# Sliding-window attention and an ELU MLP on one core: q and k turned in 32x32 squares by VectorE and gathered by DMA, v placed by GpSimd

## The chip, the core and the metric

The kernel runs on one core of one Trainium2 chip. A core has a matrix engine (TensorE, PE in the profile; its weight loads are PEld), three engines for elementwise work (VectorE or DVE, ScalarE or ACT, GpSimd or POOL), and SyncE (SP), which here only issues DMAs. Each works through its own queue in order and waits on semaphores for the others. The metric is device time in microseconds of one execution, as the median of several.

## What is computed

```python
B, H, S, D = 8, 8, 576, 64
scores = scale * np.matmul(q, k.transpose(0, 1, 3, 2))        # scale = 1/8
rel = pos[:, None] - pos[None, :]
slopes = 2.0 ** (-8.0 * (np.arange(H) + 1) / H)
bias = slopes[:, None, None] * (-np.abs(rel))[None]
mask = (rel >= 0) & (rel < 128)
scores = np.where(mask, scores + bias[None], -1e9)
attn = softmax(scores)
x = np.matmul(attn, v)                     # to 4608 x 512, heads side by side
h = x @ w_in                               # 512 x 2048
g = np.where(h > 0.0, h, np.exp(np.minimum(h, 0.0)) - 1.0)
out = g @ w_out                            # 2048 x 512
```

A query sees itself and the 127 keys before it, so a block of 128 queries needs its own block of 128 keys and the one before.

## The kernel before

All matmuls take 16-bit inputs. `q` and `k` must be laid with the head dimension on partitions for the scores, so each batch's q and k are turned. They are loaded with a cast by DMAs that GpSimd issues (`load_qk`, line 76): partition p holds the four sequence rows 4p to 4p+3 of all heads, 1 KB at a time. `transposes(b, hp)` (line 307) turns two heads of q and k at a time with eight 128x128 transposes on TensorE into one PSUM tile `tp`, and two copies of 64x1024, on VectorE for even `hp` and on ACT for odd, put them into `QK[b % 2]` (lines 322 and 324). The tile `tp` uses the same two PSUM buffers (pool `ps_s`) as the score tiles. The last 64 rows of a batch are the tail, turned by `transposes_tail` (line 327). Because of the loading by fours, a block of 128 sequence positions stands in QK in the order j, i (position 4i + j), and so do the positions of v in `VP` and the rows of the output.

Partitions 64 to 127 of `QK[i]` hold extra rows (`TQ`, `TK`) by which the same matmul adds the bias and switches off masked groups. For batch 0 a separate matmul adds bias and mask instead. The extra rows are made once during batch 0 (`terms`, `group_rows`, `k_term`) and spread over the heads by DMAs from SP (`fill`, `fill_k`).

v of batches 0 to 2 is loaded like q and k into `vs` in one DMA of 1 KB runs, and `place_v4` (line 114) moves it into `VP` on VectorE, 16 copies of 32x512 a batch. v of batches 3 to 7 is loaded by `load_v` (line 119) from SP, 16 DMAs of 64 KB and one of 128 KB a batch, in runs of 256 bytes that already stand in the right partitions, and `cast_v` (line 132) converts it on GpSimd into `VP`, five instructions a batch.

The program is laid out by hand in steps. Sixteen steps make a batch; step `s` of batch `b` (number 16b + s) runs `scores(b, s)` for one bank of scores, its exponential on ACT (line 372) and, from batch 1 on, the `cut` on VectorE (line 380), which takes the minimum with a band so that masked entries vanish. `values` multiplies the bank of the step before with v (line 394), `normalize` (lines 414 and 415) divides by the sums, and `turn` brings the result into `xT`, for batches 0 and 1 by TensorE and a VectorE copy, from batch 2 on by a DMA transpose that SP issues (line 423). Each step from 4 on also carries one `hidden` group of the MLP: matmuls into one of two PSUM buffers `hp` (line 451), the exponential on ACT (line 455), a clamp on GpSimd (line 456), and in the next step `elu` on VectorE (line 463), which also frees the `hp` buffer. Steps 36 and 37 have no `hidden`. From step 13 on a quarter of an output block follows at the end of each step (`output`, line 492; every fourth step ends in an ACT copy and stores from SP).

Within a step the order on every engine is: `hidden`, the `elu` of the step before, then the tasks listed for the step, then `output`:

```python
        for s in range(max(OUT) + 1):
            if s in HID:
                hidden(*HID[s])
            if s - 1 in HID:
                elu(*HID[s - 1])
            for f, a in tasks.get(s, []):
                f(*a)
            if s in OUT:
                output(*OUT[s])
```

For the preparation of the next batches the tasks of batch b >= 2 are (s0 = 16b): `transposes(b + 1, hp)` at s0 + 5, 9, 10, 13, the tail at s0 + 14; the loads of k and q of b + 2 at s0 + 10 and 12, their tails at 11 and 13; `load_v(b + 2, n)` at s0 + 18 + 2n and `cast_v` three steps later. For b = 1 the transposes are at s0 + 9, 10, 13, 14; for b = 0 at 14, 14, 15, 15. Hence in one steady batch VectorE has per step one `elu`, one `cut` and, in ten of sixteen steps, a normalization, GpSimd one clamp per step beside its DMA issues and casts.

The softmax here doesn't subtract the row's maximum and nothing guards it: scores larger than these inputs give would overflow.

## Time and profile before

| | us |
|---|---|
| median of 7 runs (lowest, highest) | 367.15 (366.21, 368.05) |
| profiled execution | 366.21 |
| its span, first to last instruction | 364.4 |

| longest groups (engine, line, what) | busy us | mean ns |
|---|---|---|
| PE L451, hidden matmuls, x1536 | 150.3 | 246 |
| PE L492, output matmuls, x576 | 146.4 | 379 |
| DVE L463, elu, x144 | 98.0 | 680 |
| POOL L456, clamp, x144 | 88.5 | 614 |
| ACT L455, exponential of the MLP, x144 | 86.0 | 597 |
| ACT L372, exponential of the scores, x128 | 76.0 | 593 |
| DVE L380, cut, x112 | 49.5 | 442 |
| ACT L322, copies of turned q and k, x28 | 28.1 | 1005 |
| POOL L134, casts of v, x25 | 19.5 | 779 |
| DVE L324, copies of turned q and k, x28 | 19.2 | 685 |
| PE L312, transposes of q and k, x224 | 17.1 | 219 |
| DVE L116, placing of v, x48 | 15.1 | 315 |

A row gives the engine, the line of the kernel, the time that instructions of the group were running in all, and the mean of one. Matmuls overlap each other, so the mean of one is longer than its share of the engine's time. The granted TensorE clock was 0.994 of full speed on average. The DMA engines moved 37.06 MB in 81948 packets, 51952 of them under 512 bytes; the queue of DMAs issued by GpSimd took 35.5% of the sixteen engines' time, the one of SP 25.8%.

### The profile page before, as it was taken

The page shows a single profiled execution, that of the slowest core. Times are in us where ns is not written, and L with a number is a line of the kernel's source. Part 1 is how long each engine was busy: PE and PEld are TensorE (multiplying, and loading weights), DVE is VectorE, ACT ScalarE, POOL GpSimd, SP SyncE. Part 2 cuts the span into 40 slices and gives each one's busy share as a digit, 9 for nine tenths or more (in the row PEclk, how much of TensorE's full clock was granted, in tenths as well). Part 3 has the DMA queues.
Part 4 walks back from the last instruction along what each step waited for, and adds up shares of the span by engine and source line. Part 5 has one row for each costly group of instructions (what it writes and reads, how often), then busy time and mean ns, then how long its engine had stood idle before and what let it go on. Part 6 is the DMA issues. An engine that isn't in the chain of part 4 may idle for free.

```text
span 364.4 us, 9613 instructions
## 1 busy us (share of the span) xinstructions
PE 340.4 (93%) x3790; PEld 251.7 (69%) x3790; DVE 243.5 (67%) x574; ACT 206.7 (57%) x349; POOL 145.6 (40%) x229
## 2 busy tenths in 40 slices
PE   6877997999979999999999999999999999999994
PEld 6765874777747767767777777777777777666652
DVE  6479889677886776676677767776776756634430
ACT  4364573567537655765656665676567565543431
POOL 9145624435314733472346424642443223233320
PEclk9899999999999999999999999999999999999999
DMA  8999989849244974497447945694631222211113
GB/s 115 201 205 131 207 100 177 149 91 156 41 95 91 131 112 90 106 127 112 91 106 113 131 91 107 105 142 90 96 84 45 52 47 45 50 40 48 31 43 73
DMA packets 81948, 37.06 MB, mean 102 GB/s; under 512 B 51952, under 2 KB 77296, under 8 KB 81904
## 3 DMA queue, kind: packets, MB, share of 16 engines
q0 software_dynamic: 34064, 15.40, 35.5%
q1 hardware_dynamic: 47840, 21.06, 25.8%
q8 instruction: 29, 0.48, 0.6%
q14 instruction: 15, 0.12, 0.1%
HBM read 36.70 MB, written 9.44 MB: 127 GB/s over the span
## 4 chain that ended last, share of the span: by engine, by line
PE 65%; DVE 13%; ACT 9%; DMA 7%; issue 3%; POOL 1%; SPq 0%; ACTq 0%; POOLq 0%
PE hp L451 28%; PE op L492 25%; PE sp L348 5%; ACT QK L322 5%; DVE VP L116 4%; PE av L394 3%; DMA vs<-in_v_dram 3%; DVE g L463 3%; ACT EX L372 2%; ACT e L455 2%; DMA xT<-xn 2%; DVE QK L324 1%; DVE EX L380 1%; DMA stq<-in_q_dram 1%; PE tp L312 1%
## 5 line engine op out<-in xcount | busy, mean ns | idle before, releaser
L456 POOL TENSOR_SCALAR e<-e 128x512 f32<-128x512 f32 x144 | 88.5, 614 | 201.8 <-ACT e L455 200.3
L451 PE MATMUL hp<-xT,wi 128*128 128x256 f16 (+3 forms) x1536 | 150.3, 246 | 7.9 <-DVE g L463 5.2
L451 PEld LDWEIGHTS <-wi 128*128 128x128 f16 x1536 | 121.6, 98 | 49.6 <-issue 6.9
L455 ACT ACTIVATE e<-hp 128x512 f32<-128x512 f32 x144 | 86.0, 597 | 118.0 <-PE hp L451 109.6
L492 PE MATMUL op<-wo,g 128*128 128x512 f16 x576 | 146.4, 379 | 0.0
L463 DVE SCALAR_TENSOR_TENSOR g<-e,hp 128x512 f16<-128x512 f32 x144 | 98.0, 680 | 23.9 <-POOL e L456 22.7
L380 DVE TENSOR_TENSOR EX<-EX,band 128x512 f16<-128x512 f16 x112 | 49.5, 442 | 57.2 <-ACT EX L372 57.1
L372 ACT ACTIVATE EX<-sp 128x512 f16<-128x512 f32 x128 | 76.0, 593 | 15.0 <-PE sp L368 10.5
L492 PEld LDWEIGHTS <-g 128*128 128x128 f16 x576 | 51.2, 98 | 36.9
L348 PE MATMUL sp<-QK 128*128 128x128 f16 (+3 forms) x576 | 49.8, 213 | 0.4 <-DVE QK L305 0.4
L394 PE MATMUL av<-VP,EX 128*128 128x65 f16 x576 | 38.6, 193 | 4.5 <-DVE EX L380 2.5
L394 PEld LDWEIGHTS <-EX 128*128 128x128 f16 x576 | 31.5, 98 | 9.0 <-DVE EX L380 4.0
L415 DVE TENSOR_TENSOR xn<-av,rden 128x256 f16<-128x256 f32 x80 | 34.0, 424 | 2.8
L348 PEld LDWEIGHTS <-QK 128*128 128x128 f16 (+1 forms) x576 | 31.3, 97 | 1.4 <-DVE QK L305 0.5
L496 ACT COPY ob<-op 128x512 f32<-128x512 f32 x36 | 21.1, 585 | 14.3 <-PE op L492 6.4
L322 ACT COPY QK<-tp 64x1024 f16<-64x1024 f16 x28 | 28.1, 1005 | 1.6 <-PE tp L312 1.4
L414 DVE RECIPROCAL rden<-av 128x4 f32<-128x4 f32 x80 | 14.4, 180 | 16.5 <-PE av L394 15.5
L134 POOL TENSOR_SCALAR VP<-vf 128x512 f16<-128x512 f32 (+1 forms) x25 | 19.5, 779 | 2.4 <-DMA vf<-in_v_dram 2.4
L324 DVE COPY QK<-tp 64x1024 f16<-64x1024 f16 x28 | 19.2, 685 | 1.1 <-PE tp L312 0.9
L312 PE MATMUL tp<-ident,stq 128*128 128x128 f16 x224 | 17.1, 219 | 2.3 <-ACT QK L322 1.0
L312 PEld LDWEIGHTS <-stq 128*128 128x128 f16 x224 | 13.8, 98 | 3.4 <-issue 3.2
L116 DVE COPY VP<-vs 32x512 f16<-32x512 f16 x48 | 15.1, 315 | 1.4 <-DMA vs<-in_v_dram 0.7
(70 smaller groups left out, 117.9 us busy)
## 6 DMA issues: line engine op xcount, KB each, us to landing
out_dram<-ob SPq DMA_DIRECT2D x128, 64.0 KB, 1.7
vf<-in_v_dram SPq DMA_DIRECT2D x80, 64.0 KB, 2.2
stq<-in_k_dram POOLq DMA_DIRECT2D x7, 512.0 KB, 6.4
stq<-in_q_dram POOLq DMA_DIRECT2D x7, 512.0 KB, 7.7
wi<-in_moe_w_in_dram POOLq DMA_DIRECT2D x4, 512.0 KB, 11.6
wo<-in_moe_w_out_dram POOLq DMA_DIRECT2D x4, 512.0 KB, 14.4
QK<-TQ SPq DMA_DIRECT2D x2, 576.0 KB, 8.8
vs<-in_v_dram POOLq DMA_DIRECT2D x2, 512.0 KB, 10.0
```

The source lines that it names most:

```text
L312: nc.tensor.transpose(t[:, g, w, :, j, :], stq[b][:, w, 2 * hp + g, 2 * j:2 * j + 2, :].rearrange("p a d -> p (a d)"), ident)
L322: nc.scalar.copy(o, i)
L348: nc.tensor.matmul(t[:, o:o + n], qk[0:r, h, 1, kc:kc + 128], qk[0:r, h, 0, qc:qc + n], start=b > 0 or o == 0, stop=b > 0)
L372: nc.scalar.activation(e[:, 0:512], t, AF.Exp, scale=0.125)
L380: V.tensor_tensor(out=e, in0=e, in1=band[:, c:c + n].unsqueeze(1).broadcast_to([128, 512 // n, n]), op=ALU.min)
L394: nc.tensor.matmul(a[:, l, :], e[:, c:c + 128], vp[:, n, h, 0:D + 1], start=st, stop=sp)
L415: V.tensor_tensor(out=xnt[b, i][:, 4 * half:4 * half + 4, :], in0=a[:, :, 0:D], in1=r.unsqueeze(2).broadcast_to([128, 4, D]), op=ALU.mult)
L451: nc.tensor.matmul(p[:, l * w + u0:l * w + u1], w_in_sb[:, c, fc * 128:(fc + 1) * 128], xT[:, c, x0:x0 + u1 - u0], start=(c == 0), stop=(c ...
L455: nc.scalar.activation(e, p, AF.Exp)
L456: nc.gpsimd.tensor_scalar(out=e, in0=e, scalar1=1.0, scalar2=0.0, op0=ALU.min, op1=ALU.max)
L463: V.scalar_tensor_tensor(out=gs[t][:, f0:f0 + nf, c0:c0 + w], in0=sh(es.pop((t, j))), scalar=1.0, in1=sh(hps.pop((t, j))), op0=ALU.subtrac ...
L492: nc.tensor.matmul(ops[t], gs[t][:, fc, ts * 128:(ts + 1) * 128], w_out_sb[:, fc, :], start=(fc == 0), stop=(fc == NFC - 1))
```

## The change

For batches 2 to 7 the TensorE transposes of q and k go, with their copies out of PSUM. In their place `squares` transposes on VectorE: the staged tile is turned in 32x32 squares, in eight instructions of 128x512 a batch, into a tile `tt` of which there is one buffer. `collect` then moves the squares by eight DMAs a batch from SP: for block i of 128 positions and each half of the head dimension, 32 partitions of `tt` go to 32 partitions of `QK`, q and k together, in runs of 2 KB. For that `QK` is laid out by block: `[128, 2, 5, H, 128]` instead of `[128, H, 2, 640]`, and the scores, the zero fills and the copies of the transposes that stay (batches 0 and 1, and all tails) follow it.

v of batches 3 to 7 is loaded as for batch 2 (`load_v4`, one DMA from GpSimd, and `load_v4_tail`), and `place_by_pool` moves it into `VP` on GpSimd with 16 instructions of 32x512 a batch, two a step.

The extra rows of `QK[1]` are spread over the heads by five ACT copies of 64x1024 (`fill_q`) and five VectorE copies of 32x1024 (`fill_k`) in steps 10 to 14; `QK[0]` gets its rows by one DMA from `QK[1]` at step 20, in place of three at step 22.

```diff
-    QK = [one([128, H, 2, 640], F16, f"QK{i}") for i in range(2)]
+    QK = [one([128, 2, 5, H, 128], F16, f"QK{i}") for i in range(2)]
...
-    def load_v(b, n):
-    def cast_v(b, n):
+    def place_by_pool(b, n, u):
+        for j in (2 * u, 2 * u + 1):
+            nc.gpsimd.tensor_scalar(
+                out=VP[b % 2][32 * j:32 * j + 32, n, :, 0:D], in0=vs[b][32 * n:32 * n + 32, :, j, :],
+                scalar1=1.0, scalar2=0.0, op0=ALU.mult, op1=ALU.add)
...
-        def fill(i):
-            nc.sync.dma_start(QK[i][64:128, :, 0, 0:576],
-                              TQ[64:128, :].unsqueeze(1).broadcast_to([64, H, 576]))
-            nc.sync.dma_start(QK[i][g_, :, 1, :], TK[g_, :].unsqueeze(1).broadcast_to([32, H, 640]))
-
-        def fill_k(i):
-            nc.sync.dma_start(QK[i][r_, :, 1, :], QK[1 - i][r_, :, 1, :])
+        def fill_q(n):
+            nc.scalar.copy(QK[1][64:128, 0, n, :, :],
+                           TQ[64:128, 128 * n:128 * n + 128].unsqueeze(1).broadcast_to([64, H, 128]))
+
+        def fill_k(n):
+            V.tensor_copy(QK[1][g_, 1, n, :, :],
+                          TK[g_, 128 * n:128 * n + 128].unsqueeze(1).broadcast_to([32, H, 128]))
...
+        def fill_other():
+            nc.sync.dma_start(QK[0][64:128], QK[1][64:128])
...
+        def put(t, o, by_act):
+
+            for odd in range(2):
+                (nc.scalar.copy if by_act else V.tensor_copy)(
+                    o.rearrange("p w n h (a o i) -> p w n h a o i", o=2, i=32)[:, :, :, :, :, odd, :]
+                    .rearrange("p w n h a i -> p w n (h a) i"),
+                    t[64 * odd:64 * odd + 64].rearrange("p w n h a i -> p w n (h a) i"))
...
+        def squares(b, n):
+
+            if b not in tt:
+                tt[b] = stage.tile([128, 2, 2, H, 4, 32], F16, name="tt", tag="tt", bufs=1)
+            w, dh, hs = 1 - n // 4, n // 2 % 2, slice(4 * (n % 2), 4 * (n % 2) + 4)
+            V.transpose(out=tt[b][:, w, dh, hs, :, :].rearrange("p h j i -> p (h j) i"),
+                        in_=stq[b][:, w, hs, :, 32 * dh:32 * dh + 32].rearrange("p h j d -> p (h j) d"))
+
+        def collect(b, n):
+
+            i, dh = n // 2, n % 2
+            nc.sync.dma_start(
+                QK[b % 2][32 * dh:32 * dh + 32, :, i, :, :].rearrange("p w h c -> p w (h c)"),
+                tt[b][32 * i:32 * i + 32, :, dh, :, :, :].rearrange("p w h j i -> p w (h j i)"))
...
             def mm(o, h, kc, qc, n):
-                nc.tensor.matmul(t[:, o:o + n], qk[0:r, h, 1, kc:kc + 128], qk[0:r, h, 0, qc:qc + n],
+                nc.tensor.matmul(t[:, o:o + n], qk[0:r, 1, kc, h, :], qk[0:r, 0, qc, h, 0:n],
...
-                for hp in range(NP):
-                    at(s0 + ((5, 9, 10, 13) if b > 1 else (9, 10, 13, 14) if b else (14, 14, 15, 15))[hp],
-                       transposes, b + 1, hp)
+                for hp in range(NP if b == 0 else 0):
+                    at((14, 14, 15, 15)[hp], transposes, 1, hp)
+                for n in range(8 if b else 0):
+                    at(s0 + (n if b > 1 else 6 + n // 2), squares, b + 1, n)
+                    at(s0 + (8 if b > 1 else 10) + n // 2, collect, b + 1, n)
...
-                for n in range(5):
-                    at(s0 + 18 + 2 * n, load_v, b + 2, n)
-                    at(s0 + 21 + 2 * n, cast_v, b + 2, n)
+                at(s0 + 14, load_v4, b + 2)
+                at(s0 + 19, load_v4_tail, b + 2)
+                for n in range(4):
+                    for u in range(2):
+                        at(s0 + 20 + 2 * n + u, place_by_pool, b + 2, n, u)
...
-        at(10, fill, 1)
+        for n in range(5):
+            at(10 + n, fill_q, n)
+            at(10 + n, fill_k, n)
...
-        at(22, fill, 0)
-        at(22, fill_k, 0)
+        at(20, fill_other)
```

## The prediction

> **What bounds the kernel now.** I read the page first (busy shares), then the table of stretches (how one batch compares with another), then the order in time of a few steps, then the rows of single lines.
>
> ```profile
> PE 340.4 (93%) x3790; PEld 251.7 (69%) x3790; DVE 243.5 (67%) x574; ACT 206.7 (57%) x349; POOL 145.6 (40%) x229
> ```
>
> TensorE is busy nearly always. A share of busy time doesn't say what an edit is worth, so I cut the span into stretches (length, then busy time of PE, PEld, DVE, ACT, POOL, clock, DMA):
>
> ```profile
> 36.00:51.00 15.00, 14.27 (x210) 11.59 (x209) 12.86 (x31) 9.41 (x14) 7.46 (x11) 1.00 1.26 192
> 93.00:112.30 19.30, 16.44 (x194) 11.54 (x193) 15.66 (x43) 8.99 (x16) 4.93 (x11) 1.00 0.34 71
> 209.41:246.18 36.77, 36.31 (x381) 26.73 (x379) 25.95 (x58) 23.58 (x40) 16.64 (x25) 1.00 0.66 111
> 280.79:314.46 33.67, 33.67 (x382) 25.10 (x379) 22.66 (x52) 19.90 (x37) 9.80 (x16) 1.00 0.22 50
> ```
>
> The third row is sixteen steps of the steady loop, with the transposes of one next batch in them; the fourth is sixteen steps of batch 7, which prepares no next batch. Both are bound by TensorE, and the same attention and MLP work takes 36.77 us with the preparation and 33.67 us without. The first two rows (the end of batch 0, the first half of batch 2) have idle TensorE beside a VectorE that is 86% and 81% busy.
>
> A step with transposes and a step after it, in order of time (start, length, engine, line):
>
> ```profile
> 216.68 1.04 PE L451 MATMUL hp<-xT,wi 128*128 128x256 f16 x8
> 217.90 0.61 PE L312 MATMUL tp<-ident,stq 128*128 128x128 f16 x8
> 218.34 1.03 PE L492 MATMUL op<-wo,g 128*128 128x512 f16 x4
> 218.43 0.61 POOL L456 TENSOR_SCALAR e<-e 128x512 f32<-128x512 f32 x1 [1.47 <-ACT e L455]
> 218.87 0.45 DVE L380 TENSOR_TENSOR EX<-EX,band 128x512 f16<-128x512 f16 x1 [1.03 <-ACT EX L372]
> 219.00 0.79 POOL L134 TENSOR_SCALAR VP<-vf 128x512 f16<-128x512 f32 x1
> 219.21 1.04 PE L451 MATMUL hp<-xT,wi 128*128 128x256 f16 x8
> 219.24 1.38 DVE L324 COPY QK<-tp 64x1024 f16<-64x1024 f16 x2
> 221.39 1.03 PE L451 MATMUL hp<-xT,wi 128*128 128x256 f16 x8
> ```
>
> Eight transposes hold TensorE from 217.90 to 218.34, 0.44 us (their 0.61 overlaps the next matmul). The step is 2.53 us (216.68 to 219.21) and the one after, which waits for the two copies on VectorE, 2.18. A step without either is 2.09: the ACT exponentials of the MLP (L455) start at 211.50, 213.59, 215.67, 217.75.
>
> The rows of single lines (min, median and max in ns):
>
> ```profile
> L380 DVE TENSOR_TENSOR EX<-EX,band x112: 415/448/461, 53.7 to 313.4; 128x512 f16<-128x512 f16 x112
> L134 POOL TENSOR_SCALAR VP<-vf x25: 618/789/792, 105.4 to 274.5; 128x512 f16<-128x512 f32 x20, 64x512 f16<-64x512 f32 x5
> L116 DVE COPY VP<-vs x48: 275/285/725, 9.0 to 104.5; 32x512 f16<-32x512 f16 x48
> L322 ACT COPY QK<-tp 64x1024 f16<-64x1024 f16 x28 | 28.1, 1005 | 1.6 <-PE tp L312 1.4
> vf<-in_v_dram SPq DMA_DIRECT2D x80, 64.0 KB, 2.2
> stq<-in_q_dram POOLq DMA_DIRECT2D x7, 512.0 KB, 7.7
> vs<-in_v_dram POOLq DMA_DIRECT2D x2, 512.0 KB, 10.0
> ```
>
> **What the Trainium skill says.** "VectorE: DVE Perf Modes", section "The three transpose paths", gives 311 ns for a 128x128 transpose of 2-byte data in 32x32 blocks on VectorE; the trace has none. "SBUF — State Buffer", section "Who interferes with whom": a VectorE instruction with two SBUF inputs, or in a two-port mode, and a GpSimd instruction that reads SBUF block each other, whoever starts second waits. The trace half agrees: L116, usually 0.285 us, takes up to 0.725, and the GpSimd conversion L134 takes 0.618 alone but 0.79 when it starts just after L380, as at 219.00; L380 itself never goes over 0.461 beside L456. "Perfetto Trace Analysis", section "GPSIMD Engine Instruction", advises timing GpSimd by the spacing of starts; here L134 starts 0.57 us after the L456 whose length is 0.61.
>
> **What goes.** Of batches 2 to 7, 192 transposes with 24 copies on ACT (1.005 us) and 24 on VectorE (0.685). In a steady batch that is worth 36.77 - 33.67 = 3.10, less the tail's transposes, which stay (eight of 64 columns, 0.39 us and a short wait, 0.45 together): **2.65 us**. ACT never sets the pace afterwards. The v loads of batches 3 to 7 (85 DMAs, 17 a batch) leave SP, with 25 GpSimd conversions.
>
> **What comes, part by part.**
>
> Squares: 8 VectorE transposes of 128x512 a batch, 48 in all. Estimate from the page: 311 ns plus 384 more elements at one per cycle of 0.96 GHz is 0.71; the nearest row, L463 with 512 elements, is 0.68. I take 0.70 (0.65 to 0.75). Per batch VectorE gets 5.6 and loses 4 copies, 2.7. That fits overall, but the squares come one a step in the first 8 steps. A step with a normalization holds VectorE from the cut at 210.53 to the end of the xn at 212.27, 1.74 us; with a square 2.44 against 2.09. Five of those eight steps normalize, three don't (1.13 + 0.70 = 1.83): 17.7 us of work in about 16.9. What is late then is the cut (L380), on which the next step's value matmuls wait. It has 0.35 us of idle time before it and about 0.25 after it. Price: 0.3 a batch (0 to 1).
>
> Gather: 8 DMAs a batch on SP, 128 KB each, in rows of 2 KB. Nearest rows: 64 KB in 2.2, 128 KB in 2.9. They are issued four to eight steps (8 us or more) before the first scores that read them. On SP each waits for its squares, with output stores and the xn transposes queued behind; those have several us of room and SP is rid of 17 DMAs. Taken as nothing (0 to 0.5 a batch, if the gather meets the q and k loads).
>
> Placing v: 16 GpSimd instructions of 32x512 in place of 5, two a step in steps 4 to 11 of batches 2 to 6, behind the step's L456. Behind them waits the next L456, then L463, then the matmul that reuses the hp buffer. One costs between 0.57 (spacing) and 0.79: 0.61 + 2 x 0.62 = 1.85 or 0.61 + 2 x 0.79 = 2.19 against 2.09. At the low end it fits. Added to that, in steps 10 and 11 GpSimd issues the k load (0.93) and a tail (0.72): L456 comes some 1.3 us late there. Its room is about 0.9 (the e buffer is ready at 210.70, the matmul that needs its hp starts at 212.51, L463 takes 0.68 and a start). Price 0.4 a batch (0 to 3). The mutual block: with GpSimd nearly always busy, a cut that is late because of a square finds it in a placing and waits up to 0.6; steps 4, 6 and 8 are the ones. Price 0.7 (0 to 1.5).
>
> v's load: one 512 KB DMA issued in step 14 behind k and q, used from step 20, six steps or 12.5 us later. Such loads landed in 7.4 to 12.6 us. Taken as nothing (up to 3 us a batch if late).
>
> Fills in batch 0: two fill DMAs give way to 5 ACT copies of 64x1024 (1.0 us each, from L322) and 5 VectorE copies of 32x1024 in steps 10 to 14. L274, 32x640, has a median of 0.32; I take 0.42. There VectorE is without a gap from 31.9 to 43.7, so some 1.5 of its 2.1 us shows. ACT needs 0.6 + 0.6 + 1.0 a step, and the last fill stands before the exponential of step 15, for whose bank the last transposes of batch 1 wait. Price 2.0 together (1 to 4).
>
> **Where they meet, in sum.** Batches 3 to 6, four times: -2.65 + 0.3 + 0.4 + 0.7 = -1.25, so -5.0. Batch 2 (transposes of 3 removed): its first eight steps are VectorE bound already, with four L116 placings (1.18 us) a step in four of them; squares put 2.8 there, of which 2.2 shows; removal gives 2.4 and GpSimd takes 0.4: +0.2. Batch 1: two squares a step in steps 22 to 25 make 12.6 us of VectorE work (8 x 0.70, 4 x 0.68, 4 x 0.45, two normalizations 1.2, an xT copy 0.42, a tail 0.85) where the steps took 10.3 (67.25 to 77.52); about 1.5 shows. The six steps after (77.52 to 92.92) lose three pairs or more of copies and 24 transposes: 15.4 to some 13.7. Together -0.2. Batch 0: +2.0. Total **-3.0**. The profiled execution took 366.21 us (span 364.4, 1.8 outside), the lowest of seven; the median is 367.15. So 366.2 - 3.0 is 363.2, and on the median **364.1**.
>
> **Rivals.** (1) Nearly all is covered: GpSimd runs at its low price and locks don't meet. Then batches 3 to 6 give 2.3 each, batch 2 gives 0.5, batch 1 gives 0.8, batch 0 costs 1.0: -9.5, or 357.6. For it: the TensorE bound is clear and every added engine is under 80% on average. Against: the additions are bunched. (2) Slower: GpSimd becomes the bound in steps 4 to 11. If consecutive placings are over 0.74 us apart, its step passes 2.09 and the queue never drains; with 0.79, 8 x 2.19 + 1.65 = 19.2 us stand against 16.7, and cuts lose 1.6 in blocks: 4.1, less 0.9 room, is 3.2 a batch in place of 1.1 (batch 2: 0.4). That is 4 x 2.1 + 2.8 = 11.2 more than the forecast: 375. For it: the 0.79 row. Against: that row starts inside a cut each time. (3) v lands late, as a 12.6 us landing in the trace would: GpSimd stands still, L456 behind it; 1.5 us in five batches is 371.5. (4) The start alone decides: fills cost 5 in place of 2, 367: no change. That the transposes don't leave is excluded by the diff.
>
> **Numbers.** Forecast 0.45, rivals 0.15, 0.22, 0.10 and 0.08. The forecast's own range is 361 to 367. About 0.2% is what a measurement tells from no change, so 366.4 to 367.9. The forecast lies below it in most of its share, with rival 1: 0.53 faster; parts of the forecast and rival 4: 0.10 same; the rest 0.37 slower. The range 357.5 to 374.5 leaves out the far half of rivals 1 and 2.
>
> **What would show it.** Squares in a row of about 0.70 us x48; 32 transposes left on L312's successor. Sixteen steps of a middle batch near 35.5 us: at 34.3 rival 1 is right, at 37.5 or more rival 2, and then idle TensorE waits on L463, which waits on POOL. Longer cuts than 0.46 show the block. A GpSimd wait on the v load means rival 3. The stretch from 36 to 51 shows the fills. If VectorE squares take over 0.9 us, or middle batches are slower than 36.8, the prediction is wrong.

## The result, and the profile after

| | us |
|---|---|
| before, median of 64 runs (lowest, highest) | 367.11 (365.28, 370.95) |
| after, median of 27 runs (lowest, highest) | 371.63 (368.92, 373.77) |
| after / before, 95% interval | 1.0113 (1.0094 to 1.0131) |
| profiled execution after; its span | 373.01; 371.2 |

The change makes the kernel 1.1% slower: 4.5 us on the median. The time lies in the predicted range, and the sign is the other one. A trace shows one execution alone, and the one of the kernel after took 373.01 us, 1.4 above its median; between the two profiled executions the span grew by 6.8 us where the prediction had -3.0. To see where, take the start of every sixteenth exponential of the scores (one per step) from the order in time, and subtract: that gives the length of each batch.

| us | before | after | difference | predicted |
|---|---|---|---|---|
| first exponential | 11.71 | 12.73 | +1.02 | 0 |
| batch 0 | 41.00 | 43.72 | +2.72 | +2.0 |
| batch 1 | 41.83 | 40.22 | -1.61 | -0.2 |
| batch 2 | 38.43 | 44.50 | **+6.07** | +0.2 |
| batch 3 | 37.99 | 42.63 | **+4.64** | -1.25 |
| batch 4 | 36.78 | 35.03 | -1.75 | -1.25 |
| batch 5 | 36.77 | 35.04 | -1.73 | -1.25 |
| batch 6 | 36.80 | 34.17 | -2.63 | -1.25 |

Batch 7, which prepares nothing, is as long after as before: its first fifteen steps take 31.47 us in both. Times below leave out executions over 1.5% above the fastest of their kernel (one each of squares3_two_tt, all_later, before_k_late, best and best_loads_apart); the traces of the last two are of these and not used, and the one of all_later, also of these, only shows where it waited.

The page's busy shares after:

```profile
PE 337.4 (91%) x3598; PEld 244.9 (66%) x3598; DVE 261.1 (70%) x604; ACT 189.2 (51%) x330; POOL 186.5 (50%) x291
```

TensorE has 192 instructions fewer and yet only 3 us less busy time. The table of stretches says why (length, then busy time of PE, PEld, DVE, ACT, POOL, clock, DMA share, GB/s): steps 32 to 38, the last part of batch 3, the sixteen steps of batch 4, and a stretch of batch 7.

```profile
96.67:121.41 24.74, 16.56 (x154) 10.70 (x153) 19.43 (x45) 8.02 (x16) 8.62 (x13) 0.86 0.45 63
166.38:183.80 17.42, 12.23 (x114) 8.13 (x112) 7.53 (x19) 5.13 (x11) 6.74 (x10) 0.80 1.74 140
183.80:218.83 35.03, 34.42 (x346) 24.58 (x345) 27.98 (x63) 19.80 (x38) 24.75 (x38) 1.00 0.68 107
288.04:321.20 33.16, 33.16 (x371) 24.72 (x370) 22.41 (x51) 19.39 (x37) 9.80 (x16) 1.00 0.25 51
```

The steady batch went the predicted way. In the first two rows TensorE is idle for 8.2 and 5.2 us, and its mean clock falls to 0.86 and 0.80: two stretches, each with a gap and a slow time after it.

A steady step with a square in it (start, length, engine, line):

```profile
184.40 1.04 PE L452 MATMUL hp<-xT,wi 128*128 128x256 f16 x8
184.43 0.43 DVE L381 TENSOR_TENSOR EX<-EX,band 128x512 f16<-128x512 f16 x1 [0.27 <-ACT EX L373]
184.77 0.70 DVE L318 STREAM_TRANSPOSE tt<-stq 128x512 f16<-128x512 f16 x1
...
186.49 1.04 PE L452 MATMUL hp<-xT,wi 128*128 128x256 f16 x8
```

It takes 2.09 us, as a step without transposes did before. The rows of single lines (min, median, max in ns): squares, placings by GpSimd and by VectorE, the cut, the fills.

```profile
L318 DVE STREAM_TRANSPOSE tt<-stq x48: 664/699/712, 73.5 to 269.7; 128x512 f16<-128x512 f16 x48
L122 POOL TENSOR_SCALAR VP<-vs x80: 609/616/779, 108.7 to 278.8; 32x512 f16<-32x512 f16 x80
L117 DVE COPY VP<-vs x48: 271/285/664, 9.1 to 111.9; 32x512 f16<-32x512 f16 x48
L381 DVE TENSOR_TENSOR EX<-EX,band x112: 398/449/785, 57.1 to 320.1; 128x512 f16<-128x512 f16 x112
L255 ACT COPY QK<-TQ x5: 1041/1042/1042, 38.3 to 51.1; 64x1024 f16<-64x1024 f16 x5
L259 DVE COPY QK<-TK x5: 418/419/485, 38.3 to 49.4; 32x1024 f16<-32x1024 f16 x5
```

So the prices of the new operations were right. What was wrong is where they meet something. The two places, by the longest wait of TensorE in each (total, number, longest): in batch 2 (112 to 122 us) and at the end of batch 3 (166 to 178 us).

```profile
PE av L395 <- DVE EX L381: 2.8, 1, 2.8
```

```profile
PE hp L452 <- issue: 5.2, 1, 5.2
```

The second has no releaser named. The queues of GpSimd and SP a little earlier show one (start, length of the issue):

```profile
164.62 0.93 POOL L81 DMA_DIRECT2D stq<-in_k_dram  x1
```

```profile
165.34 2.05 SPq L424 DMA_TRANSPOSE xT<-xn  x1
```

The same two in the kernel before, and the wait of TensorE for the second there:

```profile
156.18 0.95 POOL L80 DMA_DIRECT2D stq<-in_k_dram  x1
158.95 1.23 SPq L423 DMA_TRANSPOSE xT<-xn  x1
```

```profile
PE hp L451 <- DMA xT<-xn: 1.2, 1, 1.2
```

That transposing DMA brings `xT` for the `hidden` group of step 62. It landed (all its data had arrived) 9.1 us after its start; before, it took 5.6. In the kernel before, the load of k was issued 2.8 us ahead of it, now 0.7, because GpSimd's placings hold up the issue.

### The profile page after: what moved, and what is told of

Read it like the earlier page. It is cut to its first block, busy times and chain, and to the rows that moved or that the text cites. A ratio compares the mean times of both kernels' runs of the same rounds, so it can differ in the third digit from the quotient of the medians.

```text
span 371.2 us, 9293 instructions
## 1 busy us (share of the span) xinstructions
PE 337.4 (91%) x3598; PEld 244.9 (66%) x3598; DVE 261.1 (70%) x604; ACT 189.2 (51%) x330; POOL 186.5 (50%) x291
## 4 chain that ended last, share of the span: by engine, by line
PE 57%; DVE 16%; POOL 11%; DMA 6%; issue 4%; ACT 3%; SPq 1%; ACTq 0%; POOLq 0%; DVEq 0%
PE hp L452 24%; PE op L493 22%; POOL VP L122 6%; PE sp L349 5%; DMA QK<-tt 4%; DVE VP L117 4%; DVE g L464 4%; POOL e L457 4%; PE av L395 3%; DVE tt L318 2%; DMA stq<-in_q_dram 1%; DVE xn L416 1%; PE spare L506 1%; DVE EX L381 1%; ACT EX L373 1%
## 5 line engine op out<-in xcount | busy, mean ns | idle before, releaser
L457 POOL TENSOR_SCALAR e<-e 128x512 f32<-128x512 f32 x144 | 88.8, 617 | 163.4 <-ACT e L456 160.1
L452 PE MATMUL hp<-xT,wi 128*128 128x256 f16 (+3 forms) x1536 | 153.6, 249 | 16.4 <-DVE g L464 9.8
L452 PEld LDWEIGHTS <-wi 128*128 128x128 f16 x1536 | 123.2, 99 | 60.3 <-issue 14.3
L493 PE MATMUL op<-wo,g 128*128 128x512 f16 x576 | 148.5, 383 | 0.0
L373 ACT ACTIVATE EX<-sp 128x512 f16<-128x512 f32 x128 | 76.0, 594 | 19.2 <-PE sp L369 10.0
L381 DVE TENSOR_TENSOR EX<-EX,band 128x512 f16<-128x512 f16 x112 | 52.8, 472 | 35.9 <-ACT EX L373 35.6
L122 POOL TENSOR_SCALAR VP<-vs 32x512 f16<-32x512 f16 x80 | 51.4, 643 | 5.5
L318 DVE STREAM_TRANSPOSE tt<-stq 128x512 f16<-128x512 f16 x48 | 33.2, 698 | 0.9 <-DMA QK<-tt 0.9
L497 ACT COPY ob<-op 128x512 f32<-128x512 f32 x36 | 21.1, 586 | 14.8 <-DMA out_dram<-ob 5.7
L117 DVE COPY VP<-vs 32x512 f16<-32x512 f16 x48 | 17.0, 354 | 0.7
L506 PE MATMUL spare<-ident 128*128 128x128 f16 x94 | 9.9, 289 | 1.6 <-DVE ident L163 1.6
L506 PEld LDWEIGHTS <-ident 128*128 128x128 f16 x94 | 8.9, 136 | 1.7 <-DVE ident L163 1.6
L297 ACT COPY QK<-tp 64x1024 f16<-64x1024 f16 x6 | 6.0, 1007 | 6.2 <-PE tp L288 4.8
```

What stands on the lines that cost most here:

```text
L122: nc.gpsimd.tensor_scalar(out=VP[b % 2][32 * j:32 * j + 32, n, :, 0:D], in0=vs[b][32 * n:32 * n + 32, :, j, :], scalar1=1.0, scalar2=0.0, ...
L318: V.transpose(out=tt[b][:, w, dh, hs, :, :].rearrange("p h j i -> p (h j) i"), in_=stq[b][:, w, hs, :, 32 * dh:32 * dh + 32].rearrange("p ...
L373: nc.scalar.activation(e[:, 0:512], t, AF.Exp, scale=0.125)
L381: V.tensor_tensor(out=e, in0=e, in1=band[:, c:c + n].unsqueeze(1).broadcast_to([128, 512 // n, n]), op=ALU.min)
L452: nc.tensor.matmul(p[:, l * w + u0:l * w + u1], w_in_sb[:, c, fc * 128:(fc + 1) * 128], xT[:, c, x0:x0 + u1 - u0], start=(c == 0), stop=(c ...
L457: nc.gpsimd.tensor_scalar(out=e, in0=e, scalar1=1.0, scalar2=0.0, op0=ALU.min, op1=ALU.max)
```

## The experiments

Sixteen kernels. Each was timed beside the kernel before; the table gives the median, the ratio to before with its 95% interval, and, from the one profiled execution, the length of batches 2 and 3 (a dash: no trace to use). Lengths and median are of different executions: the traced one took 365.8 us in busy_gaps and 370.2 in squares3_two_tt.

| kernel | us | ratio | batch 2 | batch 3 |
|---|---|---|---|---|
| after | 371.63 | 1.0113 (1.0094 to 1.0131) | 44.5 | 42.6 |
| load5_later | 363.30 | 0.9904 (0.9865 to 0.9943) | 44.5 | 34.2 |
| collect4_later | 372.31 | 1.0140 (1.0104 to 1.0176) | 44.1 | 43.1 |
| busy_gaps | 369.71 | 1.0075 (1.0048 to 1.0102) | 42.8 | 38.0 |
| squares3_later | 377.73 | 1.0296 (1.0265 to 1.0326) | 39.2 | 52.6 |
| squares3_two_tt | 368.11 | 1.0017 (0.9992 to 1.0041) | 39.0 | 44.8 |
| all_later | 358.24 | 0.9779 (0.9715 to 0.9843) | - | - |
| dma_fills | 369.71 | 1.0067 (1.0043 to 1.0090) | 43.3 | 42.5 |
| squares_only | 385.14 | 1.0478 (1.0438 to 1.0518) | 50.1 | 47.3 |
| v_by_pool_only | 375.24 | 1.0220 (1.0182 to 1.0259) | 42.6 | 38.7 |
| fills_only | 370.26 | 1.0087 (1.0057 to 1.0117) | 38.8 | 38.4 |
| before_k_late | 365.69 | 0.9972 (0.9952 to 0.9992) | 38.4 | 36.9 |
| place3_later | 371.65 | 1.0129 (1.0086 to 1.0171) | 44.5 | 42.8 |
| best | 357.23 | 0.9748 (0.9706 to 0.9790) | - | - |
| best_place3 | 356.78 | 0.9710 (0.9682 to 0.9739) | 39.2 | 34.2 |
| best_loads_later | 354.92 | 0.9668 (0.9615 to 0.9720) | 39.1 | 34.3 |
| best_loads_apart | 355.74 | 0.9708 (0.9654 to 0.9762) | - | - |

### The stop at the end of batch 3

**load5_later** moves the loads of q and k of batch 5 behind that transpose:

```diff
-                    at(s0 + 10 + 2 * i, load_qk, b + 2, w)
-                    at(s0 + 11 + 2 * i, load_tail, b + 2, w)
+                    at(s0 + (12 + i if b == 3 else 10 + 2 * i), load_qk, b + 2, w)
+                    at(s0 + (13 + i if b == 3 else 11 + 2 * i), load_tail, b + 2, w)
```

> Changed kernel, with the k load of batch 5 two steps later (step 60 instead of 58, q at 61), so that GpSimd issues it after the DMA transpose of step 59 that step 62 waits for. Theory A1 (the transfer of k in front of the transpose is what makes it land after 9.1 us): landing under 4 us, the 5.2 us gap near 169 us and the half clock after it go, batch 3 shrinks from 42.6 us to 35 to 36, total 5 to 7 us below the changed kernel. Theory A2 (the gathers that SP issues around the transpose make it late): the gap stays, batch 3 above 40 us.

**collect4_later** moves the last four gathers of batch 4 (a gather is one DMA of `collect`), some of which stand beside the transpose on SP, two steps later (`collect` for b == 3, n > 3).

> Changed kernel, with the last four gathers of batch 4's q and k two steps later (steps 60 and 61 instead of 58 and 59), so that none of them is issued within four us before or after the DMA transpose of step 59. Theory A2 (the gathers make the transpose late): the gap near 169 us goes, batch 3 shrinks from 42.6 us to 35 to 37. Theory A1 (the k load does it): the gap stays, batch 3 within 1.5 us of 42.6.

load5_later is 8.3 us faster than the kernel after, more than theory A1 had, and 1% faster than the kernel before. The kernel collect4_later isn't faster, but it doesn't do what it was meant to: its four gathers were issued 2.1 to 4.1 us behind the start of the transpose, and all were in flight with it, where in the kernel after it was two. So what clears the gathers as the sole cause is load5_later, where two of them stand beside a transpose that landed after 3.5 us. In load5_later the stretch of the former stop (the last four steps of batch 3) has a TensorE without a gap, at full clock:

```profile
166.45:175.41 8.96, 8.96 (x114) 6.72 (x112) 7.00 (x17) 5.01 (x11) 6.77 (x10) 1.00 1.00 138
```

In collect4_later the profile names the releaser that it left out in the kernel after (waits from 166 to 178 us):

```profile
PE hp L452 <- DMA xT<-xn: 6.0, 1, 6.0
```

**squares_only** has squares and gathers, but the old v path (17 loads a batch from SP, casts by GpSimd), so no placing holds up the load of k. **v_by_pool_only** has the v part, but turns q and k of all batches by TensorE, so there are no gathers.

> The change without its v part: v of batches 3 to 7 loaded by 17 DMAs a batch from SP and cast by GpSimd as before; squares, gathers, layout and fills as in the kernel after. Nothing is left out. Theory A (GpSimd's placings delayed the k load of batch 5 until it stood beside the transpose of xT): without them GpSimd issues it early in step 58, the stop of steps 62 and 63 is gone and batch 3 is 34 to 36 us, while batch 2 stays at 43 to 45 (its squares meet VectorE's placings of v of batch 2, which are there in both): 371.6 - 7.5 = 364, range 362.5 to 366.5. Rival A3 (the gathers on SP alone delay the transpose, or collide with the v loads on SP): batch 3 stays above 40 us and the time above 368.

> The change without its squares and gathers: q and k of all batches turned by TensorE and copied as before, in the new layout, with the fills by ACT and VectorE, and v of batches 3 to 7 loaded in 1 KB runs and placed by GpSimd. Nothing is left out. Theory S (batch 2 lost 6.1 us because the squares of batch 3 stand beside VectorE's placings of v of batch 2): with neither there, batch 2 is 38 to 40 us. In batch 3 the placings delay the k load as in the kernel after, but the transpose of xT isn't behind gathers on SP; if the k load still stands within 3 us of it, batch 3 is over 40 us, else 37 to 38.5. Batches 4 to 6 keep their transposes: 36.5 to 37.5. Sum 369 to 374. Rival S2 (GpSimd's placings themselves cost batch 2 through the lock with VectorE): batch 2 stays above 43 us.

squares_only is almost 19 us above its range, on the side of its rival. Without the placings the load of k is early, but the transposes themselves are late: on SP they stand behind gathers, v loads and output stores. A load of *q* now stands 0.4 (batch 2) and 3.6 us (batch 3) ahead of them, and TensorE stops in both batches (batch 3's wait, from 180 to 196 us):

```profile
PE hp L471 <- DMA xT<-xn: 10.1, 1, 10.1
```

v_by_pool_only, with a load of k 1.1 us ahead and no gathers, has a transpose that lands after 6.0 us; TensorE waits 1.5 us for it, and batch 3 is 38.7. The load does stand within 3 us, for which over 40 us was expected: a load ahead isn't enough for the long stop. Its batch 2 (42.6) lies between the two theories; that is taken up below. The time is 1.2 above its range.

**before_k_late** is the kernel before with one number changed, the k load of batch 5 in step 59 in place of 58.

> The kernel before, with one edit: GpSimd issues the load of k of batch 5 in step 59 in place of step 58, some 2.2 us later. Nothing is left out. Theory M (a transposing DMA of xT that is issued within some 8 us behind a load of q, k or v lands late, and a load directly ahead of it is worst): the transpose of step 59 lands after 8 to 9.5 us in place of 5.6, TensorE stops for 3 to 4 us before the hidden group of step 62, its clock is halved after that, and the kernel goes from 367.2 to 371 to 375 us though nothing of the change is in it. Rival M2 (the stop needs the change's gathers on the DMA engines too): the transpose lands within 6.5 us and the time stays within 1 us of the kernel before.

Theory M missed both its numbers. The step is the right one, but GpSimd issued the load 0.4 us *behind* the start of the transpose, at 159.97 against 159.56, not ahead of it. The transpose landed in 4.2 us, batch 3 became 1.1 us shorter and the kernel 1.3 us faster than the kernel before beside it (366.96). It shows, in a kernel without the change, that this transpose and this load are in each other's way and that their order decides; that a load directly ahead stops TensorE without gathers was not produced. The transpose of step 59 in these kernels:

| kernel | last load of q, k or v ahead of it | gathers in flight with it | landed after us |
|---|---|---|---|
| before_k_late | over 30 us | 0 | 4.2 |
| load5_later | 27.6 us | 2 | 3.5 |
| before | 2.8 us | 0 | 5.6 |
| v_by_pool_only | 1.1 us | 0 | 6.0 |
| busy_gaps | 0.7 us | 2 | 7.1 |
| collect4_later | 2.2 us | 4 | 8.3 |
| squares_only | 3.6 us | 4 | 8.4 |
| after | 0.7 us | 2 | 9.1 |

A load ahead costs some 2 us, load and gathers together 4 to 6, gathers alone nothing. These are single executions: busy_gaps and the kernel after have nearly the same neighbours and differ by 2 us, and why is open. The MLP can bear about 4 us there: in the kernel after TensorE ran dry at 169.3, 4.0 us after the start of the transpose. In batches 4 and 5 transposes landed after 7.3 and 7.2 us and stopped nothing: a batch yields 4.5 blocks of 128 rows and the MLP uses 4 in sixteen steps, so it falls half a block further behind in each batch.

### The clock behind a gap

**busy_gaps** puts idle matmuls where TensorE waits (25 in step 35, 40 in step 36, 60 in step 61), into a spare bank:

```diff
+        def keep_busy(n):
+            t = ps_x.tile([128, 256], F32, name="busy", tag="xps")
+            for _ in range(n):
+                nc.tensor.matmul(t[:, 0:128], ident, ident, start=True, stop=True)
...
+        at(35, keep_busy, 25)
+        at(36, keep_busy, 40)
+        at(61, keep_busy, 60)
```

> Changed kernel, with idle matmuls (identity by identity into an unused bank) at the places where TensorE stood still: 25 in step 35, 40 in step 36, 60 in step 61, some 55 ns each. They add nothing to the output. Theory C (half of the loss is the clock, which falls to half after a gap and stays there for 3.4 to 6.8 us): the waits themselves stay as long, but the rows of the clock show no 0.5 near 113 and 175 us; batch 2 and batch 3 shrink by 2 to 3 us each, total 4 to 6 us below the changed kernel. Theory D (the clock is independent of the gaps, or the waits alone are the loss): total the same or up to 2 us above.

With 125 matmuls *more* the kernel is 1.9 us faster, which is less than theory C had and not what D had (the intervals of the two ratios just touch). The same two stretches, in the kernel after:

```profile
105.00:122.00 17.00, 11.77 (x93) 7.32 (x94) 12.48 (x28) 5.14 (x9) 6.29 (x10) 0.80 0.23 41
165.00:178.00 13.00, 7.81 (x86) 5.54 (x84) 4.48 (x11) 3.36 (x6) 6.78 (x11) 0.85 1.95 133
```

and in busy_gaps:

```profile
105.00:122.00 17.00, 16.07 (x192) 12.11 (x190) 14.74 (x31) 7.40 (x14) 9.39 (x15) 1.00 0.29 54
165.00:178.00 13.00, 13.00 (x179) 10.55 (x177) 7.73 (x19) 5.01 (x9) 6.48 (x10) 1.00 1.29 159
```

In these two stretches the clock stays at 1.00. Against the trace of the kernel after, batch 2 gains 1.7 us and batch 3 gains 4.6, of which 2.0 is a transpose that landed after 7.1 us in place of 9.1, so the clock is at most 2.6. But this trace is of the fastest of eight executions, 3.9 us below the median; how much of the 1.9 us on the median is the clock in each place isn't shown.

The Trainium skill states the mechanism ("TensorE: Matmul & The Clock Gate", section "What's actually happening"): the clock is halved after an idle window of about 3.4 us. The trace agrees on the half, but the window need not be idle. The clock of the kernel after fell at 112.6 us, and that of busy_gaps at 100.5, ahead of its first filled gap. The 3.4 us before the fall, and the time after it, in the kernel after:

```profile
109.15:112.55 3.40, 1.38 (x12) 0.65 (x12) 3.31 (x8) 1.18 (x2) 2.14 (x4) 1.00 0.30 19
112.60:119.30 6.70, 5.41 (x30) 3.33 (x31) 3.47 (x9) 1.69 (x3) 0.39 (x1) 0.50 0.16 39
```

and in busy_gaps:

```profile
97.10:100.50 3.40, 1.42 (x21) 1.01 (x19) 3.18 (x8) 0.90 (x3) 1.34 (x2) 0.99 1.07 180
100.50:103.90 3.40, 3.40 (x28) 2.66 (x26) 3.28 (x10) 0.98 (x3) 0.08 (x1) 0.50 0.23 15
```

TensorE was busy for 41 and 42% of the 3.4 us, and up to the fall no single wait in batch 2 had lasted over 2.3 us in the one and 2.0 in the other.

### Batch 2

**squares3_later** moves the squares of batch 3 by four steps (36 to 43), past VectorE's placings of v of batch 2 (32 to 35), and the gathers to steps 44 to 47.

```diff
-                    at(s0 + (n if b > 1 else 6 + n // 2), squares, b + 1, n)
-                    at(s0 + (8 if b > 1 else 10) + n // 2, collect, b + 1, n)
+                    at(s0 + (n + 4 if b == 2 else n if b > 1 else 6 + n // 2), squares, b + 1, n)
+                    at(s0 + (12 if b == 2 else 8 if b > 1 else 10) + n // 2, collect, b + 1, n)
```

> Changed kernel, with the squares of batch 3 four steps later (steps 36 to 43 instead of 32 to 39) and their gathers in steps 44 to 47, so that they no longer share steps 32 to 35 with the four VectorE placings of v a step. Theory A (the loss of batch 2 is VectorE overfilled in those four steps, plus the half clock of TensorE that follows its idle gaps): the 16 steps of batch 2 shrink from 44.5 us to 38.5 to 40, the half clock near 113 us goes, total 4 to 6 us below the changed kernel, about 367. Theory B (VectorE work costs the same wherever it stands, because TensorE waits for it anyway): batch 2 stays at 43 us or more, total within 1.5 us of the changed kernel.

Batch 2 shrank by 5.3 us, as expected, but batch 3 grew by 10, so that the time rose by 6.1 where it was to fall. The waits from 141 to 148 us:

```profile
PEld L452 <- DVE g L464: 7.8, 1, 7.8
DVE tt L318 <- DMA QK<-tt: 7.7, 1, 7.7
```

The first square of batch 4 writes the only buffer `tt`, which the last gathers of batch 3 still read; they landed up to 9.3 us after their issue, behind a load of v. The `elu` queued behind that square on VectorE is what TensorE waits for. **squares3_two_tt** has a second buffer (`bufs=2`).

> The kernel after with the squares of batch 3 at steps 36 to 43 and its gathers at 44 to 47, as in squares3_later, and a second buffer for the turned squares tt. Nothing is left out. In squares3_later the first square of batch 4 waited 7.7 us for the last gathers of batch 3, which landed up to 9.3 us after their issue, with the elu queued behind it on VectorE. Theory B1 (this wait, by the single buffer, is the whole cost of the move): batch 3 goes from 52.6 back to 42.6 us or less (the stop of steps 62 and 63 stays), batch 2 stays near 39.2, so 371.6 - 5.3 = 366.3, range 364.5 to 368.5. Rival B2 (the gathers of batch 3 that land late stop the scores of batch 3 as well, or the late squares push VectorE): batch 3 stays above 46 us and the time above 370.

The 7.7 us wait is gone and the time is in its range. Batch 3 is 2.2 us above the kernel after, though, between the two branches: TensorE waits 1.7 us for a transpose at 147.6 us, and 5.7 in place of 5.2 at the old stop. The transposes of steps 46 and 48 landed after 8.5 and 9.2 us behind the loads of v and q of batch 4 (8.1 and 7.2 in the kernel after).

**place3_later** leaves the squares and moves only GpSimd's placings of v of batch 3, from steps 36 to 43 to 38 to 45.

```diff
-                        at(s0 + 20 + 2 * n + u, place_by_pool, b + 2, n, u)
+                        at(s0 + (22 if b == 1 else 20) + 2 * n + u, place_by_pool, b + 2, n, u)
```

> The kernel after with one edit: GpSimd's placings of v of batch 3 in steps 38 to 45 in place of 36 to 43. Nothing is left out. Theory L (in step 35 GpSimd's first four placings run beside VectorE's last four, and the two block each other: the four copies took 1.94 us in place of 1.49, 2.25 in v_by_pool_only; that wait and the half clock behind it are part of batch 2's loss): the copies of step 35 keep to 0.29 each, batch 2 goes from 44.5 to 41.5 to 43 us and the time from 371.6 to 368.5 to 370.5. Rival L2 (the squares alone carry the loss; a gap of TensorE stays long enough to halve its clock): batch 2 stays within 0.5 us of 44.5.

The last four of VectorE's placings in the kernel after, and in place3_later (start, length of the four together):

```profile
110.29 1.94 DVE L117 COPY VP<-vs 32x512 f16<-32x512 f16 x4
```

```profile
108.45 1.19 DVE L117 COPY VP<-vs 32x512 f16<-32x512 f16 x4
```

In squares3_two_tt the four take 2.26 us, in v_by_pool_only 2.25. This is the mutual block that the prediction took from the Trainium skill ("SBUF — State Buffer", section "Who interferes with whom"), with up to 0.66 us for a copy of 0.29. Four kernels make a square of it. Steps 32 to 38 take (best_place3 differs in other edits too, outside these steps but for one load of v):

| us | GpSimd's placings beside VectorE's | two steps later |
|---|---|---|
| squares in steps 32 to 39 | 24.7 (after) | 22.6 (place3_later) |
| squares in steps 36 to 43 | 19.2 (squares3_two_tt) | 16.8 (best_place3) |

Early squares cost 5.5 to 5.8 us, the block 2.1 to 2.4, the clock included in both; before, these steps took 17.2. Three of the four, place3_later, squares3_two_tt and best_place3, show how the costs divide (the row of the kernel after is the first in the table of stretches above):

```profile
94.99:117.58 22.59, 15.31 (x154) 10.09 (x153) 18.52 (x45) 7.90 (x15) 5.95 (x9) 0.92 0.45 65
```

```profile
97.06:116.25 19.19, 15.26 (x154) 10.07 (x153) 15.89 (x41) 7.91 (x16) 8.09 (x13) 0.91 0.54 81
```

```profile
93.44:110.20 16.76, 13.90 (x154) 9.46 (x153) 14.81 (x41) 7.90 (x15) 5.67 (x9) 1.00 0.58 89
```

Length less busy time is TensorE's idle time. The early squares add 4.3 to 4.4 us of idle time, and 1.3 to 1.4 of busy time with the same 154 matmuls, at a lower clock; the block adds 0.9 to 1.1 idle and 1.3 to 1.4 busy. So the clock is over half of the block's cost and a quarter of the squares'. Only four squares (2.8 us of VectorE work) leave these steps when the squares are moved. They also push VectorE's copies beside GpSimd's clamps: in squares_only, where GpSimd places nothing, copies of steps 32 to 34 took 0.69, 0.60 and 0.60 us.

Each does harm alone as well. v_by_pool_only, with the block and no squares, needs 21.1 us for these steps, which is most of what its batch 2 lost; squares_only needs 21.9.

And yet place3_later's batch 2 is as long as before, the number that its rival L2 had: it gained 2.1 us in steps 32 to 38 and lost them again in steps 44 to 47 (11.5 us in place of 9.4). GpSimd's queue there (start, length):

```profile
127.33 0.61 POOL L457 TENSOR_SCALAR e<-e 128x512 f32<-128x512 f32 x1
128.02 1.29 POOL L122 TENSOR_SCALAR VP<-vs 32x512 f16<-32x512 f16 x2
129.37 0.72 POOL L102 DMA_DIRECT2D stt<-in_k_dram  x1
130.16 0.61 POOL L457 TENSOR_SCALAR e<-e 128x512 f32<-128x512 f32 x1
130.85 1.45 POOL L122 TENSOR_SCALAR VP<-vs 32x512 f16<-32x512 f16 x2
132.36 0.94 POOL L81 DMA_DIRECT2D stq<-in_q_dram  x1
133.38 0.60 POOL L457 TENSOR_SCALAR e<-e 128x512 f32<-128x512 f32 x1
```

A step with two placings and a DMA issue takes GpSimd 2.8 to 3.2 us (start of one L457 to the next) where TensorE needs 2.09. The late placings meet the loads of k and q in four steps in place of two. That this queue is what costs the 2 us isn't shown: best_loads_apart, below, takes two of the loads out of it and isn't faster.

### The start

**dma_fills** gives the fills of `QK[1]` back to DMAs from SP (ten of them), all in step 10; **fills_only** is the kernel before with the new layout and the new fills and nothing else.

> The kernel after with the rows of QK[1] spread by DMAs from SP in step 10, as before, in place of ACT and VectorE copies; the rest is the change. Nothing is left out. Theory C1 (the copies themselves cost what batch 0 lost): batch 0 goes from 43.7 to about 41.0 and the time falls by 2.7 to 369. Rival C2 (batch 0 is longer for the new layout, through the copies of turned q and k in 1024-element pieces with another order, and not for the fills): batch 0 stays above 43 and the time within 0.7 of the kernel after.

> The kernel before with the new layout of QK, its extra rows spread by ACT and VectorE copies; q, k and v otherwise as in the kernel before. Nothing is left out. The start alone: batch 0 at 43.7 us as in the kernel after, the other batches as in the kernel before, so 367.2 + 2.7 + 1.0 for the later start = 369 to 371. If the later start of each batch also shifts loads against the transposes of xT, another batch changes by over 1 us.

dma_fills: batch 0 goes from 43.72 to 41.96, the time falls by 1.9, 0.8 to 1.0 short of the expectation. fills_only: batch 0 at 43.0, and the time as expected; batch 3 is 0.4 longer. The fills are most of the cost, though about 1 us of batch 0 remains (the layout, or the spread of single executions, which is 42.7 to 44.0 in kernels with the same start; open). The later first exponential isn't the change's: it stood at 12.38 in before_k_late, which differs from the kernel before only from step 58 on, and at 10.78 in fills_only.

### Together

**all_later** is load5_later with the late squares and two `tt`. **best** adds dma_fills and the load of v of batch 4 in step 38 in place of 46. **best_place3** adds place3_later.

> load5_later (the loads of q and k of batch 5 in steps 60 to 63) together with the late squares of batch 3 and the second buffer tt. Nothing is left out. If the two losses are separate, they add: load5_later's batches (43.7, 40.2, 44.5, 34.2, 35.0, 35.0, 34.2) with 39.2 in place of 44.5, so 363.3 - 5.3 = 358.0, range 356.5 to 360. If the loss of batch 2 only wanders on to batch 3, as it did in squares3_later, batch 3 is above 37 us and the time stays at 361 or more.

> all_later with two more edits: the load of v of batch 4 in step 38 in place of 46, ahead of the loads of k and q, and the rows of QK[1] spread by DMAs from SP in step 10 as in dma_fills. Nothing is left out. In all_later the transposes of xT of steps 47 and 48 landed after 10.1 and 9.5 us, 2.5 and 5.2 us behind that load of v, and TensorE stopped for 3 us. By theory M they land in under 6 us now and batch 3 is 34 to 35.5 us in every run; the fills bring 1.8: 363.3 - 5.5 - 1.9 = 355.9, range 354.5 to 358. If the load of v only moves the trouble to the transpose of step 41, batch 2 is above 41 us and the time above 358.

> The kernel best (median 357.6) with the placings of v of batch 3 two steps later as in place3_later. Nothing is left out. With the squares of batch 3 in steps 36 to 43 the placings are the only thing left beside VectorE's copies in step 35, so theory L has its largest effect here: steps 35 and 36 lose no more to the block, the clock isn't halved, and batch 2 goes from 39 to 36.5 to 37.5 us: 355 to 356.5. By L2 no change: 357 to 358.

all_later came out on its point (358.2 for 358.0), from three executions between 358.1 and 362.4. In its slowest, the one traced, the load of v of batch 4 stood 2.5 us ahead of a transpose, which landed after 10.1 us, and TensorE waited 3.0. best moved that load and came out 1.3 above its point, within its range. best_place3 is 0.3 above its range, between the two branches: the block is gone (16.8 us in the square above), but steps 44 to 47 (12.0 us) give back what steps 32 to 38 gain, as in place3_later; batch 2 is at 39.2.

**best_loads_later** moves the loads of batches 6 and 7 two steps, as load5_later does for 5 (`b > 2`). **best_loads_apart** also issues those of batch 4 in steps 36 and 37.

> best_place3 with the loads of q and k of batches 6 and 7 in steps 76 to 79 and 92 to 95 as well, two steps behind the last placings, as load5_later has it for batch 5. Nothing is left out. Theory Q (GpSimd's queue: in steps 10 and 11 of a batch two placings, a clamp and a DMA issue last longer than the step, and that is the part of batches 4 and 5 by which they stand above batch 6 and above batch 3 of load5_later, 35.03 against 34.17): batches 4 and 5 go from 35.1 to 34.2 to 34.4 us, the time from 356.8 to 355.1, range 354.3 to 356. Rival Q2 (the difference is the transposing DMA's later landing, or nothing of the queue): batches 4 and 5 stay at 35.0 and the time within 0.5 of 356.8.

> best_loads_later with the loads of k and q of batch 4 in steps 36 and 37, where GpSimd has nothing else, in place of 42 and 44. Nothing is left out. In best_place3 GpSimd is without a gap from 119.7 to 130.8 us, with those loads among the placings, and TensorE waits 2.5 us for elu behind it. By theory Q this goes: batch 2 from 39.2 to 36.5 to 37.5 us and the time to 353 to 354. By what the loads did to transposes elsewhere, those of steps 37 to 42 can land 7 to 9 us after their issue instead; if the MLP needs one sooner, batch 2 stays at 38.5 us or more and the time at 354.5 or above.

In best_loads_later batches 4 and 5 take 34.11 and 34.12 us (35.09 in best_place3), and TensorE has no gap in the sixteen steps of batch 4:

```profile
167.36:201.47 34.11, 34.11 (x346) 24.54 (x345) 28.75 (x63) 19.80 (x37) 24.77 (x38) 1.00 0.86 133
```

It beats both kernels: 354.92 us, 3.3% under the kernel before. best_loads_apart brings nothing more (355.7 where 353 to 354 was expected), so the gain that theory Q had for batch 2 didn't come; what batch 2 still loses is left open.

## Why the prediction was wrong

**Prices.** The squares (0.70 us predicted, 0.699 measured), the fills on ACT and VectorE (1.0 and 0.42; 1.04 and 0.42) were right, and GpSimd's placing took the low price (0.62 of 0.57 to 0.79), which removes rival 2 as it was put. Batch 0's +2.0 was right in size: without the copies (dma_fills) it is 1.8 us shorter, and about 1 us of the trace's +2.7 has another cause.

**The gain in steady batches** was right and even too small. "2.65 us" for the transposes: 36.77 before, 34.11 in best_loads_later, is 2.66. So squares, locks on the cut and placings (0.3, 0.7 and a part of 0.4) cost nothing once GpSimd's loads stand apart from the placings; the cuts did take up to 0.79 us, and TensorE had no gap. As the change puts them, batches 4 and 5 gained 1.75 where -1.25 was forecast; the difference to 2.66 is the queue of steps 10 and 11, 0.9 us in place of 0.4, the one term of that sum that was real.

**The step that failed in batch 3** is the line on the gathers, "those have several us of room and SP is rid of 17 DMAs. Taken as nothing". The room was about 4 us, the transpose landed 9.1 us after its start, and the load of k, which the same text saw come late on GpSimd, had moved directly ahead of it. The prediction saw that a gather can meet the loads (0 to 0.5 a batch), but took the landing of the transposes as given, and never asked what a load that is issued later does to them on the DMA engines. With the loads moved batch 3 takes 34.2 us, 8.5 less, of which some 0.9 is GpSimd's queue: more than the whole loss of 4.5 on the median.

**The step that failed in batch 2** is "squares put 2.8 there, of which 2.2 shows". The stretch was seen to be bound by VectorE, and the mechanism was right; but the term was mis-sized. These four squares, 2.8 us of work, cost 5.5 to 5.8 in place of 2.2: 4.3 to 4.4 in waits of TensorE and 1.3 to 1.4 in the half clock behind them, which the prediction has nowhere. The second term was missing: the block was priced on the cuts of batches 3 to 6, where it cost nothing, and not on VectorE's placings of batch 2 (2.1 to 2.4). Instead "GpSimd takes 0.4" stood there.

**Batch 1** was too dear: the squares' 1.5 us of late VectorE work didn't show. Steps 22 to 25 took 9.76 us (10.27 before). That the time still lies inside 357.5 to 374.5 is luck in part: in the traces batches 2 and 3 came out 11.8 us above the forecast, the start 1.7 above, and batches 1 and 4 to 6 came out 3.8 below it.

**The rivals.** None was the cause. Rival 3 had the right kind of mechanism (a transfer that lands late) with the wrong transfer: in the kernel after no placing waited for v; in the traced execution of all_later one did, for 4.0 us. With the loads of batch 5 and the squares of batch 3 moved, the change is worth more than the forecast's -3.0: all_later, with the new fills and the block still in it, stands at 0.9779 of the kernel before, some 8 us (5.8 to 10.5 by its interval).

## What to carry to other kernels

When work moves from one queue to another, list every DMA whose issue shifts, and lay it against the latency-critical transfers of the *other* queues: here 2 us of shift in one load cost over 7 us, and moving two loads by two steps won it back. Price a TensorE gap with the slower clock that can follow it. Give an engine that issues loads no second job in the very steps of the loads.

## What the runs showed of the hardware that was not expected

- In the sixteen traces used, 480 DMA transposes. With no load of q, k or v in flight at its start, one landed after 2.3 to 4.4 us, with gathers beside it (80 of 326) or without; two alone took longer, 5.9 and 6.3 us, with a load issued at most 0.2 us behind the start. With one load issued up to 3 us ahead it took 4.7 to 6.5 us without gathers and 6.8 to 9.6 with them; with two such loads in flight 5.7 to 8.9 and 6.7 to 10.1. A load issued 0.4 to 1 us behind its start didn't hold it up (3.7 to 4.4 us).
- The TensorE clock halved with no single gap over 2.0 us before it (busy_gaps, batch 2), behind 3.4 us of which TensorE was busy for 42%. It stayed halved for 3.4 us there and for 6.8 in the kernel after. 125 idle matmuls that fill other gaps make the kernel 1.9 us faster.
- VectorE copies of 32x512 in fp16 beside GpSimd placings of the same shape took up to 0.66 us in place of 0.285, and four of them 2.26 in place of 1.19; beside clamps of 128x512 in fp32 up to 0.69 (squares_only). Cuts took up to 0.785 in place of 0.449, and the steady step still kept its 2.09.
